# Attention with decay and two MLPs on one core: pairs 1 and 3 with p split in fp16, the low part of p's small row blocks on GpSimd, and v's bound by sums on ScalarE

## The chip, the cores and the metric

The kernel runs on one NeuronCore of a Trainium2 chip. The metric is the device time of one execution in microseconds (us), the median of several. Five engines work beside each other, each through its own queue in order: TensorE (PE in the profile; PEld is its weight load), VectorE (DVE), ScalarE (ACT), GpSimd (POOL) and SyncE (SP), which here only issues DMA transfers. An instruction that has to wait for another engine or a DMA holds up all that stands behind it on its own engine.

## The reference

```python
# q, k, v: (4 batches, 8 heads, 576 positions, 64); f: (4, 8, 576)
scores = q @ k.T / 8 + cum[:, None] - cum[None, :]     # cum: running sum of log f
attn   = softmax(causal(scores))                       # the kernel calls this p
x      = (attn @ v), heads side by side                # (2304, 512)
h      = x @ w_in;  g = max(h, 0) + alpha * min(h, 0); x = g @ w_out       # 512 -> 2048 -> 512
out    = ((x @ w_a) * (x @ w_b)) @ w_o                                     # 512 -> 1536 -> 512
```

## The kernel before

The 32 heads go through attention one after the other, two heads to a pair. A head's 576 rows of scores are four row blocks of 128 (numbered 0 to 3, with 128, 256, 384 and 512 columns because of the mask) and a rest of 64 rows, which both heads of a pair share (number 4, tile `sr`). A loop over u (line 645) goes through a list of operations: scores and softmax of head u (`s0` to `s3`, `R` for the rest), the scaling of p of head u - 1 by the softmax's sum (`h0` to `h4`) and what follows on it (`l0` to `l4`), and the products with v of head u - 2 (`p0`, `p1`). `T` makes q and k of head u + 1 ready, `vs` and `vm` work on v, `W` prepares one weight of the first MLP, and `M` takes a piece of the first MLP of an earlier batch. The MLP's matmuls are named h (with w_in) and y (with w_out); w_in and w_out come as 16 weights, one after the other through one raw tile `wr` and one tile `wx`: a DMA, then ACT (line 132), three operations on DVE (134 to 136), a cast on ACT and a subtraction on POOL.

From this list of operations a scheduler makes the order of every engine, from its own estimate of what is ready when. So a change of one operation moves others too.

Heads 0 to 9 (`NATIVE = 10`) work in f32: p is scaled in place (`p_hi`, line 461), PE transposes it block by block through PSUM (line 483), ACT and DVE copy the result out (line 237 or 235), and PE multiplies it with v in f32 (`pv_whole`, line 532). Heads 10 to 31 split p into two fp16 parts: POOL or ACT writes the high part (line 472 or 474), DVE the low part, s times ri minus the high part (line 554), DMAs transpose both (line 561), and PE multiplies them with v (lines 575 and 576), which was itself scaled and split into two fp16 parts by three operations of POOL (`split_v`, lines 325 to 327). The scale of v is one power of two for each batch, from a bound on v's absolute values: two loads of half a batch into one tile `vc` (line 334), DVE's maximum over each (line 338), and a chain over DVE, POOL (`vb`, line 345), PE (347) and DVE (348 to 353). Batch 0 is heads 0 to 7, all in f32, so this is done for batches 1 to 3 only, in the last three heads of the batch before.

Behind the heads, from about 378 us, come the rest of the first MLP and the second MLP.

Of the kernel before, what the change touches and what calls it, by code (L numbers as in the profile page):

```python
# [13 lines left out]
AF = mybir.ActivationFunctionType  # L14
ALU = mybir.AluOpType
# [33 lines left out]
    ws=[0, 1, 2, 3, 4, 5, 6, 7, 7, 8, 8, 9, 9, 10, 10, 11],  # L49
# [11 lines left out]
NATIVE = _P.get("native", 0)  # L61

# [24 lines left out]
def decay_attention_then_two_mlps(ctx, tc, q, k, v, f, w_in, w_out, alpha, w_a, w_b, w_o, out):  # L87
# [77 lines left out]
    ap_ = {"u": 0}  # L165
# [145 lines left out]
    def load_v(n):  # L311
        b, h = divmod(n, H)
        vs = ap_["vs", n % 3]
        i = 3 if n < NATIVE and n % 2 == 0 else 1
        sp.dma_start(vs[:, 0:4, i], v[b, h, 0:ST].rearrange("(t p) d -> p t d", p=128))
        sp.dma_start(vs[0:SR, 4, i], v[b, h, ST:])

    def split_v(n):

        if n < NATIVE:  # L320
            return
        vs = ap_["vs", n % 3]
        t = halves(n)
        scale = ap_["vm", (n // H) % 2][:, 1:2]
        pool.tensor_scalar(vs[:, :, 2], vs[:, :, 1], scale, 1.0, op0=ALU.mult, op1=ALU.mult)
        pool.tensor_scalar(t[:, :, 0:D], vs[:, :, 2], 1.0, 0.0, op0=ALU.mult, op1=ALU.add)
        pool.tensor_tensor(t[:, :, D:], vs[:, :, 2], t[:, :, 0:D], op=ALU.subtract)
# [8 lines left out]
    def batch_max(b, i):  # L336
        m = ap_["vm", b % 2][:, i:i + 1]
        dve.tensor_reduce(m, ap_["vc"], axis=mybir.AxisListType.X, op=ALU.max, apply_absolute_value=True)
# [55 lines left out]
    def s_view(n, i):  # L394
        if i == 4:
            return ap_["sr"]
        o = {3: 0, 2: 512, 1: 896, 0: 1152}[i]
        return ap_["s", n % 2][:, o:o + 128 * (i + 1)]
# [47 lines left out]
    p16 = {}  # L446

# [3 lines left out]
    def p_hi(n, i):  # L451

        g, o = GROUP[i]
        if n < NATIVE:
            s = s_view(n, i)
            ri = ap_["rir"][:, 0:1] if i == 4 else ap_["ri", n % 2][:, i:i + 1]
            e = eng(f"h{i}", "pool")
            if e is act:
                act.activation(s, s, AF.Copy, scale=ri)
            else:  # L460
                e.tensor_scalar(s, s, ri, 1.0, op0=ALU.mult, op1=ALU.mult)
            return
        if (n, g) not in p16:
            p16[n, g] = ap_["a"].tile(
                [128, GSIZE[g], 128], F16, tag=f"p16_{g}", name=f"p16_{n}_{g}", bufs=_P.get("p16", {}).get(g, 1),
            ), []
        t = p16[n, g][0][:, o:o + 2 * i + 2]
        s = s_view(n, i).rearrange("p (t n) -> p t n", n=128)
        ri = ap_["rir"][:, 0:1] if i == 4 else ap_["ri", n % 2][:, i:i + 1]
        e = eng(f"h{i}", "pool")  # L470
# [4 lines left out]
        p16[n, i] = t, s, ri  # L475

# [72 lines left out]
    def p_lo(n, i):  # L549
        if n < NATIVE:  # L550
            return p_whole(n, i)
        t, s, ri = p16.pop((n, i))
        g, o = GROUP[i]
        eng(f"l{i}", "dve").scalar_tensor_tensor(t[:, 1::2, :], s, ri, t[:, 0::2, :], op0=ALU.mult, op1=ALU.subtract)
        whole, done_ = p16[n, g]
        done_.append(i)
        if g == "r" or len(done_) == 2:
# [3 lines left out]
            sp.dma_start_transpose(out=PT[n, g], in_=whole.rearrange("p t n -> p (t n)"))  # L561
            del p16[n, g]

    def pv(u, c):

        if u < NATIVE:
            return pv_whole(u, c)
# [67 lines left out]
    def attention():  # L635
# [7 lines left out]
        load_qk(2)  # L643
        yield "W", -1
        for u in range(NI + LAG):
            ap_["u"] = u
            for op in order(u):
# [31 lines left out]
                elif op == "vm":  # L679
                    b = u // H + 1  # L680
                    if b < B and u % H >= H - 3:
                        i = u % H - (H - 3)
                        if i:
                            batch_max(b, i - 1)
                        if i < 2:
                            load_batch_v(b, i)
                        else:
# [430 lines left out]
```

## Time and profile before

| | us |
|---|---|
| median of 3 runs (lowest to highest) | 1076.65 (1076.21 to 1079.2) |
| profiled execution | 1079.26 |
| its span, first to last instruction | 1077.5 |

| engine | busy, share of the span |
|---|---|
| PE | 95% |
| PEld | 88% |
| DVE | 67% |
| POOL | 47% |
| ACT | 46% |

The profile is of one execution. Busy time is the time in which an engine has at least one instruction under way; matmuls overlap each other, so the duration of one is longer than its distance to the next. In the profile's names buffer numbers are left out.

### The profile page before, as it was taken

Reading aid. Unit: us, or ns where it says so; the run is one execution under the profiler, and the core shown is the slowest. Engines: PE = TensorE matmul, PEld = TensorE weight load, DVE = VectorE, ACT = ScalarE, POOL = GpSimd, SP = SyncE. Lnnn points to the kernel's source line nnn. Section 1 sums busy time; section 2 is a strip of 40 time slices with the busy share of each in tenths; the row PEclk is TensorE's granted clock in tenths of the full one; section 3 lists DMA queues with packets and bytes.
Section 4 is the critical chain, followed back from the end, with each engine's and each line's share of the span. In section 5 each row is a group of like instructions: output and inputs, shape, how many; then the busy total and the mean of one; then the engine's idle time right before and its main releaser. Section 6 shows DMA issues by size and latency. Waiting matters only on the chain.

```text
span 1077.5 us, 18303 instructions
## 1 busy us (share of the span) xinstructions
PE 1018.3 (95%) x6256; PEld 953.1 (88%) x6256; DVE 723.6 (67%) x1544; ACT 492.4 (46%) x1204; POOL 505.2 (47%) x593
## 2 busy tenths in 40 slices
PE   5899978999999999999999996999999999999998
PEld 3778868999988899999999995899989999899997
DVE  6667998698988836244467666755986558974553
ACT  6677776788777745333344443322433113321110
POOL 4334675576756745233356857522444224541111
PEclk9989988999999999999999998899999999999999
DMA  5655678596597485476767997626327383454623
GB/s 113 176 138 147 189 145 156 112 210 139 112 214 128 94 290 161 161 236 227 250 216 271 358 355 263 252 94 254 108 88 281 129 308 122 137 184 159 244 81 114
DMA packets 222561, 199.79 MB, mean 185 GB/s; under 512 B 139076, under 2 KB 195908, under 8 KB 222468
## 3 DMA queue, kind: packets, MB, share of 16 engines
q1 hardware_dynamic: 222468, 198.62, 61.0%
q8 instruction: 49, 0.80, 0.3%
q14 instruction: 44, 0.36, 0.1%
HBM read 130.37 MB, written 50.17 MB: 168 GB/s over the span
## 4 chain that ended last, share of the span: by engine, by line
PE 50%; DVE 7%; issue 3%; DMA 3%; POOL 2%; ACT 2%; DVEq 0%; ACTq 0%; POOLq 0%; SPq 0%
PE p L710 7%; PE p L712 7%; PE p L711 7%; PE o L712 4%; PE o L711 4%; PE o L710 4%; PE ya L711 3%; PE hb L712 3%; PE hb L710 3%; PE hb L711 3%; PE ya L712 3%; PE ya L710 3%; DMA wr_in<-in_moe_w_in 1%; POOL yhl L917 1%; DVE wx_a L135 1%
## 5 line engine op out<-in xcount | busy, mean ns | idle before, releaser
L710 PE MATMUL p<-yq,w_h 128*128 128x384 f32 x360 | 122.7, 341 | 7.9 <-ACT w_h L140 6.4
L711 PE MATMUL p<-yq,w_h 128*128 128x384 f32 x360 | 122.2, 339 | 0.0
L712 PE MATMUL p<-yq,w_h 128*128 128x384 f32 x360 | 121.5, 338 | 0.0
L1051 POOL TENSOR_TENSOR gg<-tc,gg 128x384 fp32r<-128x384 f32 x36 | 37.0, 1028 | 113.6 <-ACT gg L1050 103.3
L710 PE MATMUL o<-w_o,gg 128*128 128x512 f32 x216 | 84.8, 394 | 4.7 <-ACT gg L1050 4.7
L711 PE MATMUL o<-w_o,gg 128*128 128x512 f32 x216 | 85.1, 394 | 0.0
L712 PE MATMUL o<-w_o,gg 128*128 128x512 f32 x216 | 84.5, 395 | 0.0
L420 ACT ACTIVATE s<-s,nm 128x512 f32<-128x512 f32 (+3 forms) x128 | 71.4, 558 | 21.7 <-DVE nm L419 21.4
L1051 POOL TENSOR_TENSOR gg<-td,gg 128x384 fp32r<-128x384 f32 x36 | 37.2, 1035 | 93.7 <-ACT gg L1050 88.0
L710 PE MATMUL h<-xh,w_in 128*128 128x288 f32 x256 | 77.4, 306 | 2.8 <-DVE lt L705 2.8
L707 POOL TENSOR_TENSOR gb<-lt,gb 128x384 fp32r<-128x384 f32 x48 | 50.0, 1042 | 63.6 <-ACT gb L706 63.6
L710 PEld LDWEIGHTS p<-yq,w_h 128*128 128x128 f32 x360 | 68.1, 189 | 12.4 <-ACT w_h L140 6.9
L710 PE MATMUL y<-g,w_out 128*128 128x288 f32 x256 | 77.1, 306 | 1.1 <-DVE lt L705 0.9
L711 PE MATMUL y<-g,w_out 128*128 128x288 f32 x256 | 76.2, 300 | 1.2 <-POOL g L707 1.2
L705 DVE SCALAR_TENSOR_TENSOR lt<-lu,nal,hb 128x384 f32<-128x384 f32 x48 | 29.3, 611 | 70.8 <-ACT lu L704 69.2
L712 PE MATMUL h<-xh,w_in 128*128 128x288 f32 x256 | 75.5, 296 | 0.0
L711 PE MATMUL h<-xl,w_in 128*128 128x288 f32 x256 | 75.4, 295 | 0.0
L712 PE MATMUL y<-g,w_out 128*128 128x288 f32 x256 | 75.0, 299 | 0.0
L1050 ACT CAST gg<-tc 128x384 fp32r<-128x384 f32 x36 | 18.5, 514 | 123.4 <-DVE tc L1049 122.9
L711 PEld LDWEIGHTS p<-yq,w_h 128*128 128x128 f32 x360 | 68.2, 189 | 3.5
L419 DVE CUSTOM_DVE_ANT_0 s<-sc,maskz 128x512 f32<-128x512 f32 (+3 forms) x128 | 59.8, 485 | 16.2 <-PE sc L403 14.1
L712 PEld LDWEIGHTS p<-yq,w_h 128*128 128x128 f32 x360 | 67.8, 188 | 0.2
(216 smaller groups left out, 3261.6 us busy)
## 6 DMA issues: line engine op xcount, KB each, us to landing
yq<-yq_d SPq DMA_DIRECT2D x49, 768.0 KB
yq_d<-yhl SPq DMA_DIRECT2D x42, 384.0 KB
yl<-ya_d SPq DMA_DIRECT2D x48, 192.0 KB
po_d<-os SPq DMA_DIRECT2D x36, 256.0 KB
os<-po_d SPq DMA_DIRECT2D x36, 256.0 KB
wr_in<-in_moe_w_in SPq DMA_DIRECT2D x16, 512.0 KB
wr_out<-in_moe_w_out SPq DMA_DIRECT2D x16, 512.0 KB
wr_a<-in_moe_w_a SPq DMA_DIRECT2D x12, 512.0 KB
```

What stands on the lines that cost most here:

```text
L135: dve.scalar_tensor_tensor(x, high, -2 ** 31, x, op0=ALU.bitwise_and, op1=ALU.bitwise_or)
L419: dve.tensor_tensor_reduce(s, o, m, -0.125, 3.0e38, ALU.add, ALU.min, nm)
L420: act.activation(s, s, AF.Exp, bias=nm, scale=-1.0, accum_out=sm)
L705: dve.scalar_tensor_tensor(t, u, nal[:, fi:fi + 1], hp[:, :n], op0=ALU.mult, op1=ALU.add)
L707: pool.tensor_tensor(gl, t, f32(gh), op=ALU.subtract)
L710: pe.matmul(o, lh, rh, start=start, stop=False)
L711: pe.matmul(o, lh, rl, start=False, stop=False)
L712: pe.matmul(o, ll, rh, start=False, stop=stop)
L917: pool.tensor_tensor(yh[:, 1], x, f32(yh[:, 0]), op=ALU.subtract)
L1050: ap_["last"] = act.copy(g[:, 0], o).ins
L1051: pool.tensor_tensor(g[:, 1], o, f32(g[:, 0]), op=ALU.subtract)
```

## The change

Five edits. `whole(n)` says which heads stay in f32: of the first ten now only pairs 0, 2 and 4 (heads 0, 1, 4, 5, 8, 9), while pairs 1 and 3 (heads 2, 3, 6, 7) take p and v in fp16; their scores stay in f32. In all heads that are split, the low part of row blocks 0 and 1 goes from DVE to POOL: POOL scales both in place (two operations, as before, but written to s), copies both at once to the high part (384 columns) and subtracts both at once; s is laid out so that the two blocks lie side by side. The bound on v is now the sum of absolute values along each row, made by ACT (1152 columns with an accumulated sum, in place), not a maximum on DVE. Batch 0 gets one too, loaded ahead of the loop and finished in the first two heads. And the second weight of step 7 moves to step 8, with the later ones behind it.

```diff
-    ws=[0, 1, 2, 3, 4, 5, 6, 7, 7, 8, 8, 9, 9, 10, 10, 11],
+    ws=[0, 1, 2, 3, 4, 5, 6, 7, 8, 8, 9, 9, 10, 10, 11, 11],
...
+def whole(n):
+
+    return n < NATIVE and n // 2 % 2 == 0
...
     def split_v(n):
 
-        if n < NATIVE:
+        if whole(n):
             return
...
-    def batch_max(b, i):
-        m = ap_["vm", b % 2][:, i:i + 1]
-        dve.tensor_reduce(m, ap_["vc"], axis=mybir.AxisListType.X, op=ALU.max, apply_absolute_value=True)
+    def batch_bound(b, i):
+        c = ap_["vc"]
+        act.activation(c, c, AF.Abs, accum_out=ap_["vm", b % 2][:, i:i + 1])
...
-        o = {3: 0, 2: 512, 1: 896, 0: 1152}[i]
+        o = {3: 0, 2: 512, 0: 896, 1: 1024}[i]
...
+        if g == "lo":
+            pool.tensor_scalar(s, s, ri, 1.0, op0=ALU.mult, op1=ALU.mult)
+            p16[n, i] = None
+            low_done[n] = low_done.get(n, 0) + 1
+            if low_done[n] == 2:
+                dup(pool, p16[n, g][0][:, 0::2, :], lo_view(n))
+            return
...
+    def lo_view(n):
+        return ap_["s", n % 2][:, 896:1280].rearrange("p (t n) -> p t n", n=128)
...
-        eng(f"l{i}", "dve").scalar_tensor_tensor(t[:, 1::2, :], s, ri, t[:, 0::2, :], op0=ALU.mult, op1=ALU.subtract)
...
+        if g != "lo":
+            t, s, ri = got
+            dve.scalar_tensor_tensor(t[:, 1::2, :], s, ri, t[:, 0::2, :], op0=ALU.mult, op1=ALU.subtract)
+        elif len(done_) == 2:
+            pool.tensor_tensor(parts[:, 1::2, :], lo_view(n), parts[:, 0::2, :], op=ALU.subtract)
...
         stack(0)
         warm_up(_P.get("wu", [0, 0])[1], "b")
         load_qk(2)
+        load_batch_v(0, 0)
...
-                    b = u // H + 1
-                    if b < B and u % H >= H - 3:
-                        i = u % H - (H - 3)
-                        if i:
-                            batch_max(b, i - 1)
-                        if i < 2:
+                    for b in range(B):
+                        i = u - 8 * b + 3 if b else u + 1
+                        if i in (1, 2):
+                            batch_bound(b, i - 1)
+                        if i in (0, 1):
                             load_batch_v(b, i)
```

What the scheduler makes of it shows at three places. In the names the first number is the head (s_0 and s_1 are the two tiles of scores, used in turn). First ACT at the start, behind the softmax of head 0: the scaling of its row block 2, the rest's exponential (sr), the copy of the transposed p (PT32), the copies of q and k of head 2 (N_0), and head 1's exponentials. Before:

```order
L459 ACTIVATE s_0_151<-s_0_151,ri_0_154 128x384
L439 ACTIVATE sr_164,smr_167<-sr_164,nmr_166 128x576
L235 COPY PT32_0_hi_283<-tp_0_2_0_284 128x3x128
L235 COPY N_0_103<-tqk_2_0_290 64x288 x2
L235 COPY N_0_103<-tqk_2_1_296 64x288 x2
L420 ACTIVATE s_1_160,sm_1_162<-s_1_160,nm_1_161 128x512
L132 ACTIVATE wx_in0_252<-wr_in0_250 128x512
```

And now, to the same exponential of head 1 (vc's sums are those with 1152 columns):

```order
L344 ACTIVATE vc_178,vm_0_180<-vc_178 128x1152
L445 ACTIVATE sr_164,smr_167<-sr_164,nmr_166 128x576
L138 ACTIVATE wx_in0_255<-wr_in0_253 128x512
L344 ACTIVATE vc_178,vm_0_180<-vc_178 128x1152
L146 CAST w_in0_260<-wx_in0_255 128x512
L241 COPY PT32_0_hi_296<-tp_0_2_0_297 128x3x128
L241 COPY N_0_103<-tqk_2_0_303 64x288 x2
L241 COPY N_0_103<-tqk_2_1_309 64x288 x2
L138 ACTIVATE wx_in1_348<-wr_in1_346 128x512
L241 COPY PT32_0_lo_330<-tp_0_0_0_331 128x384
L344 ACTIVATE vc_178,vm_1_181<-vc_178 128x1152
L426 ACTIVATE s_1_160,sm_1_162<-s_1_160,nm_1_161 128x512
```

Three sums over vc, two weights' first steps and a cast now stand ahead of head 1's first exponential. On PE at the same place (scr: the rest's scores, tp: transposes of p, tqk: transposes of q and k), now:

```order
L409 MATMUL scr_1_1_271<-N_1_108 128x288
L353 MATMUL vm_0_289<-ident_90,vb_179 128x128
L498 MATMUL tp_0_2_0_297<-ident_90,s_0_151 128x128 x3
L378 MATMUL tqk_2_0_303<-ident_90,qkn_2_198 128x96 x3
L378 MATMUL tqk_2_1_309<-ident_90,qkn_2_198 128x96 x3
L498 MATMUL tp_0_3_3_315<-ident_90,s_0_151 128x128 x4
L409 MATMUL sc_1_3_321<-N_1_108 128x512
```

The second row, the transpose of batch 0's bound, is the new one; the others stood in the same order before. The second place is POOL in head 25's step, with p of head 24 and v of head 25 (vs). Before:

```order
L474 TENSOR_SCALAR p16_24_hi_3869<-s_0_151,ri_0_154 128x4x128
L474 TENSOR_SCALAR p16_24_lo_3872<-s_0_151,ri_0_154 128x128
L474 TENSOR_SCALAR p16_24_lo_3872<-s_0_151,ri_0_154 128x2x128
L325 TENSOR_SCALAR vs_1_172<-vs_1_172,vm_1_181 128x5x64
L326 TENSOR_SCALAR vs_1_172<-vs_1_172 128x5x64
L327 TENSOR_TENSOR vs_1_172<-vs_1_172 128x5x64
```

And now:

```order
L475 TENSOR_SCALAR s_0_151<-s_0_151,ri_0_154 128x128
L475 TENSOR_SCALAR s_0_151<-s_0_151,ri_0_154 128x256
L486 TENSOR_SCALAR p16_24_hi_3918<-s_0_151,ri_0_154 128x4x128
L245 TENSOR_SCALAR p16_24_lo_3921<-s_0_151 128x3x128
L575 TENSOR_TENSOR p16_24_lo_3921<-s_0_151,p16_24_lo_3921 128x3x128
L331 TENSOR_SCALAR vs_1_172<-vs_1_172,vm_1_181 128x5x64
L332 TENSOR_SCALAR vs_1_172<-vs_1_172 128x5x64
L333 TENSOR_TENSOR vs_1_172<-vs_1_172 128x5x64
```

Two rows more, and they stand ahead of v's. The third place is PE around the widest scores of head 16 (sc_16_3), with the first MLP's second matmuls (y, the first number is the batch, the second the half of it). Before:

```order
L711 MATMUL y_0_288_0_2280<-g_0_288_1895,w_out5_1365 128x288
L712 MATMUL y_0_288_0_2280<-g_0_288_1895,w_out5_1365 128x288
L710 MATMUL y_0_288_0_2280<-g_0_288_1895,w_out6_1375 128x288
L406 MATMUL sc_16_3_2353<-U1_0_147,T1_0_146 128x512
L407 MATMUL sc_16_3_2353<-TU2_0_148 128x512
```

And now:

```order
L412 MATMUL sc_16_3_2403<-U1_0_147,T1_0_146 128x512
L413 MATMUL sc_16_3_2403<-TU2_0_148 128x512
L729 MATMUL y_0_0_0_1611<-g_0_0_1259,w_out7_1593 128x288
L730 MATMUL y_0_0_0_1611<-g_0_0_1259,w_out7_1593 128x288
L729 MATMUL y_0_0_1_1696<-g_0_0_1259,w_out7_1593 128x288
```

At this point the MLP was in the second half of batch 0 and is now still in the first, at its last weight, w_out7; the order has it nearly level again at head 18 (408 of the MLP's matmuls ahead of that head's widest scores before, 404 now).

## Rows read from the trace of the kernel before

**Rows 1.** Stretches (us): length, busy (x instructions) by engine, granted clock, DMA share, GB/s.

```profile
14.00:108.00 94.00, 85.00 (x488) 68.66 (x486) 62.06 (x194) 66.85 (x181) 32.24 (x46) 0.95 0.59 156
108.00:152.00 44.00, 38.32 (x284) 35.48 (x283) 40.43 (x114) 34.20 (x101) 31.93 (x45) 1.00 0.68 174
152.00:175.00 23.00, 18.15 (x108) 15.41 (x108) 20.33 (x58) 16.76 (x45) 13.47 (x19) 0.63 0.75 152
175.00:220.00 45.00, 43.24 (x358) 41.99 (x357) 33.29 (x92) 30.52 (x87) 27.19 (x41) 1.00 0.65 131
220.00:378.00 158.00, 149.29 (x1248) 140.92 (x1246) 135.27 (x370) 121.65 (x343) 108.48 (x160) 1.00 0.70 148
378.00:1077.00 699.00, 680.75 (x3774) 648.79 (x3772) 422.88 (x702) 216.77 (x439) 281.88 (x256) 0.99 0.59 206
```

**Rows 2.** Timeline, 15 to 25 us: start, length, engine, line, operation, idle before.

```profile
15.76 2.61 SPq L222 DMA_DIRECT2D cum_d<-rows  x4
...
19.68 0.59 SPq L128 DMA_DIRECT2D wr_in<-in_moe_w_in  x1
...
19.68 0.55 PE L483 MATMUL tp<-ident,s 128*128 128x128 f32 x3 [0.59 <-ACT s L459]
...
22.80 0.72 ACT L420 ACTIVATE s<-s,nm 128x512 f32<-128x512 f32 x1
...
24.51 0.66 ACT L132 ACTIVATE wx_in<-wr_in 128x512 f32<-128x512 f32 x1 [0.89 <-DMA wr_in<-in_moe_w_in]
```

**Rows 3.** Timeline, 38 to 52 us: loads of vc and their readers.

```profile
38.48 0.59 SPq L334 DMA_DIRECT2D vc<-in_v  x1
...
45.09 1.35 DVE L338 TENSOR_REDUCE vm<-vc 128x1 f32<-128x1152 f32 x1 [0.54 <-DMA vc<-in_v]
...
46.47 0.35 SPq L334 DMA_DIRECT2D vc<-in_v  x1
...
50.70 1.35 DVE L338 TENSOR_REDUCE vm<-vc 128x1 f32<-128x1152 f32 x1 [1.22 <-DMA vc<-in_v]
```

**Rows 4.** Timeline of PE: f32 head at 34 us, fp16 head at 254 us.

```profile
34.12 0.93 PE L483 MATMUL tp<-ident,s 128*128 128x128 f32 x7
34.88 2.11 PE L403 MATMUL scr<-N 128*128 128x288 f32 x8
36.82 0.82 PE L532 MATMUL pvw<-PT_lo,vs 128*128 128x256 f32 x4
37.48 1.68 PE L532 MATMUL pvw<-PT_hi,vs 128*128 128x256 f32 x8
38.99 1.23 PE L532 MATMUL pvw<-PT_r,vs 128*128 128x64 f32 x10
...
253.92 0.28 PE L575 MATMUL pv<-PT_lo,vs 128*128 128x256 f16 x1
...
255.65 0.38 PE L710 MATMUL y<-g,w_out 128*128 128x288 f32 x1
```

**Rows 5.** Groups, 110:390: count, busy, mean ns; last row: ns least, median, most.

```profile
L554 DVE SCALAR_TENSOR_TENSOR p_lo<-s,ri,p_lo 128x128 f16<-128x128 f32 x22 | 12.2, 554 | 0.4 <-POOL p_lo L474 0.3
L554 DVE SCALAR_TENSOR_TENSOR p_lo<-s,ri,p_lo 128x256 f16<-128x256 f32 x22 | 12.1, 550 | 0.0
L327 POOL TENSOR_TENSOR vs<-vs 128x320 f16<-128x320 f32 x22 | 18.8, 855 | 1.2
L326 POOL TENSOR_SCALAR vs<-vs 128x320 f16<-128x320 f32 x22 | 11.0, 501 | 1.2
...
L554 DVE SCALAR_TENSOR_TENSOR p_lo<-s,ri,p_lo x44: 331/487/1137, 131.3 to 374.9; 128x128 f16<-128x128 f32 x22, 128x256 f16<-128x256 f32 x22
```

**Rows 6.** Waits of PE, 110:385: us in total, times, longest.

```profile
PE h L710 <- DVE lt L705: 2.8, 4, 1.8
PE pv L575 <- DVE nm L419: 2.8, 6, 0.6
```

**Rows 7.** Timeline of DVE: the first softmax step of head 9.

```profile
108.30 0.69 DVE L419 CUSTOM_DVE_ANT_0 s<-sc,maskz 128x512 f32<-128x512 f32 x1
```

More of the change, by code (lines that the diff above doesn't have):

```diff
@@ L313, in load_v @@
         vs = ap_["vs", n % 3]
-        i = 3 if n < NATIVE and n % 2 == 0 else 1
+        i = 3 if whole(n) and n % 2 == 0 else 1
         sp.dma_start(vs[:, 0:4, i], v[b, h, 0:ST].rearrange("(t p) d -> p t d", p=128))
@@ L446, in decay_attention_then_two_mlps @@
     p16 = {}
+    low_done = {}
     GROUP = {0: ("lo", 0), 1: ("lo", 2), 2: ("hi", 0), 3: ("hi", 6), 4: ("r", 0)}
@@ L453, in p_hi @@
         g, o = GROUP[i]
[L454 to L457, printed above, removed]
+        s = s_view(n, i)
+        ri = ap_["rir"][:, 0:1] if i == 4 else ap_["ri", n % 2][:, i:i + 1]
+        e = eng(f"h{i}", "pool")
+        if whole(n):
             if e is act:
@@ L466, in p_hi @@
             ), []
+        if g == "lo":
[5 more added lines that the diff above has]
+            return
         t = p16[n, g][0][:, o:o + 2 * i + 2]
-        s = s_view(n, i).rearrange("p (t n) -> p t n", n=128)
-        ri = ap_["rir"][:, 0:1] if i == 4 else ap_["ri", n % 2][:, i:i + 1]
-        e = eng(f"h{i}", "pool")
+        s = s.rearrange("p (t n) -> p t n", n=128)
         if e is act:
@@ L549, in p_lo @@
     def p_lo(n, i):
-        if n < NATIVE:
+        if whole(n):
             return p_whole(n, i)
-        t, s, ri = p16.pop((n, i))
         g, o = GROUP[i]
-        eng(f"l{i}", "dve").scalar_tensor_tensor(t[:, 1::2, :], s, ri, t[:, 0::2, :], op0=ALU.mult, op1=ALU.subtract)
-        whole, done_ = p16[n, g]
+        parts, done_ = p16[n, g]
         done_.append(i)
+        got = p16.pop((n, i))
+        if g != "lo":
[3 more added lines that the diff above has]
+            pool.tensor_tensor(parts[:, 1::2, :], lo_view(n), parts[:, 0::2, :], op=ALU.subtract)
         if g == "r" or len(done_) == 2:
@@ L560, in p_lo @@
             )
-            sp.dma_start_transpose(out=PT[n, g], in_=whole.rearrange("p t n -> p (t n)"))
+            sp.dma_start_transpose(out=PT[n, g], in_=parts.rearrange("p t n -> p (t n)"))
             del p16[n, g]
     def pv(u, c):
-        if u < NATIVE:
+        if whole(u):
             return pv_whole(u, c)
@@ L679, in attention @@
                 elif op == "vm":
-                    b = u // H + 1
-                    if b < B and u % H >= H - 3:
-                        i = u % H - (H - 3)
-                        if i:
-                            batch_max(b, i - 1)
-                        if i < 2:
+                    for b in range(B):
[3 more added lines that the diff above has]
+                        if i in (0, 1):
                             load_batch_v(b, i)
-                        else:
+                        if i == 2:
                             batch_scale(b)
```

## The prediction

> **What bounds the kernel now.** I read the table of stretches first [rows 1]. TensorE (PE) is busy 681 of the last 699 us, which the change leaves alone, and 85 of 94 us in the stretch of the first ten heads. So PE sets the end, and a change pays by taking work from PE or by closing its gaps. The gaps lie ahead of 220 us: 9.0 us in 14:108, 5.7 in 108:152, 4.9 in 152:175 at a granted clock of 0.63 (between the two levels 1.2 and 2.4 GHz), and 8.7 in 220:378. In that last stretch VectorE (DVE) is busy 86% and in 108:152 92%, more than any other engine beside PE, and where PE waits behind 110 us, DVE is named eight times in the list, with the MLP's lt and the softmax's nm ahead [rows 6]. In 14:108 it is another picture: DVE 66%, ScalarE (ACT) 71%, GpSimd (POOL) 34%.
>
> **The change part by part.** All sums are against the profiled execution, span 1077.5 us, 1079.26 with what lies around it. The median of the runs is 1076.65, 2.6 less, so I carry the difference over to the median.
>
> *1. v's bound for the first batch, at the start.* Pairs 1 and 3 need v scaled, so batch 0 needs a bound, and its chain now stands ahead of head 0's transposes on PE and ahead of their evictions on ACT, as the pieces above show. I follow it by rows. The first load of vc takes the place on the DMA queue where the four cum_d issues began, 15.76 [rows 2]. From issue to its reader such a load took 6.61 us once (38.48 to 45.09) and 4.23 another time (46.47 to 50.70) [rows 3]. I take 4.2, as the start has less traffic, and keep 6.6 as the end. So ACT can read at 20.0. The sum of 1152 columns isn't in the trace: the nearest row is the exponential of 512 columns with its sum, 0.72 [rows 2], which scaled up gives 1.6, and 0.72 itself is the lower end; I take 1.5. The second load goes into the same tile, so it is issued at 21.5, lands at 25.7 and is summed by 27.2. DVE's maximum, POOL's vb and PE's transpose of it add some 1 us. Head 0's transposes, at 19.68 now [rows 2], then begin at 28.2: 8.5 us later, by 6.6-us loads 13.
>
> It goes on behind that. The first weight took from its issue at 19.68 to ACT's read at 24.51, 4.8 us [rows 2]. Its successor shares the one raw tile, so it is issued when DVE is done with the first (about 27.5) and is read at 32.3. ACT's row for it now stands ahead of head 1's exponentials, and so does the third load of vc (batch 1's), which is issued only after vb is read, at about 28.5 to 30, and is summed at 34 to 36. Head 1's first exponential, at 22.80 now [rows 2], comes at about 36. PE has nothing else to do in that time. Term: **+13**, bounds +8.5 (what stands behind catches up) and +18 (both long loads).
>
> *2. Pairs 1 and 3 in fp16.* Off PE per head: ten transposes and half of a pair's five, at 0.109 us (seven in 34.12 to 34.88), 1.36 us; and the f32 products with v, 0.66 + 1.51 + 1.23 = 3.40 us [rows 4]. On PE per head: the fp16 products of a head, from 253.92 to 255.65, 1.73 us with two products of the MLP (some 0.35 us) between them, so 1.38 us [rows 4]. Four heads: 4 x (1.36 + 3.40 - 1.38) = 13.5 us. It is not all kept, since the other engines have to go faster to let PE use it. From head 1's exponential (22.80) to head 9's first softmax (108.30 [rows 7]) are 85.5 us. ACT's share of 71% makes 61 us of work there, and about four of the seven new sums that stand ahead of head 9's softmax fall behind head 1's, 6 us: 67 us. In 72 us that would be 93% of an engine that works in order, in 77 us 87%, which is what DVE reaches in 220:378. So I credit 9 us of it. Term: **-9**, bounds 0 and -13.5. POOL's additions in these heads (three operations on v, the subtractions for x) lie in an engine that is idle for two thirds; if that cover were gone they would cost what stands in part 3.
>
> *3. The low part of row blocks 0 and 1.* DVE loses 44 operations behind 108 us, 12.2 + 12.1 = 24.3 us [rows 5], 1.1 us per head. POOL gets two operations on 384 columns per head; by the 320-column ones of 0.855 and 0.501 us [rows 5] they cost 1.03 + 0.60 = 1.6 us, 36 us in 22 heads. POOL is busy 181 of the 270 us from 108 to 378 [rows 1], so it comes to 80%. In 220:378 fourteen heads free 15 us of DVE against PE's 8.7 us of gaps. DVE is not the releaser of all of them (a DMA, ACT and POOL are others), so I take **-5** there, bounds 0 and -8.7. In 108:152 three split heads free 3.3 us of DVE, but one weight more is prepared there: **-2**, bounds +1 and -4.
>
> The shared port speaks against this part. On DVE the low parts took 331 ns at best, 487 in the middle and 1137 at worst, and the mean of 128 columns is no less than that of 256 (554 and 550 ns) [rows 5], so something other than their size makes them long. The Trainium skill, SBUF — State Buffer, section Who interferes with whom, says that a DVE instruction with two inputs in SBUF contends with a GpSimd instruction that reads SBUF and that the second to issue waits until the first is done. The spread fits that rule, though no row here shows who was met. By it POOL's 1.6 us more per head of SBUF reading meets the large low parts that stay on DVE; the change removes two meetings per head and lengthens others, and where the rule takes all, the term is rival D.
>
> *4. Weights and the first MLP's second half.* In the changed order the products with w_out7 stand behind head 16's first score, in the old one 142 products of the MLP stand ahead of it; before, the thin heads are 13 and 14, now 13 to 15. The stretch 152:175 is such heads: 4.85 us idle, and at a clock of 0.63 another 18.15 x 0.37 = 6.7 us, so 5.8 per head. One more thin head is +5.8; thin heads run at DVE's pace, which is 1.1 us shorter for each of three. Term: **+3**, bounds 0 and +6.
>
> Sum: 13 - 9 - 5 - 2 + 3 = 0. The change moves the time by about nothing: a long stall is bought at the start and paid back piece by piece.
>
> **The rivals.**
> B, the stall is paid back in full. For it: PE's 13.5 us are certain, and PE was the fullest engine in 14:108. Against it: ACT's 93%. With +10 for the start, -13.5 for PE, -10 for part 3 and 0 for part 4 the sum is -13.5: 1063 us.
> C, ACT becomes the bound of the first ten heads. Place: ACT's queue, where each sum waits for a load of vc and each weight for its DMA with exponentials queued behind, and DVE's softmax and PE's scores wait for those. For it: the rows of head 1 above; against it: ACT's idle 29% now. Price: start +15, only 4 of the 13.5 us kept, -3 in the later heads, +4 in the thin ones, together +12: 1088.5 us. It decides from the point where ACT is over some 90% busy between the starts of heads 1 and 9.
> D, what DVE gains behind 108 us is lost to the shared port or to POOL's longer queue, ahead of the MLP's subtractions. The two terms of part 3 go to 0: 1083.5 us. For it: the maxima of the low parts; against it: POOL at 80%, not above.
>
> **How the numbers follow.** A, the forecast, 0.46: 1076.5 us, its own range 1070 to 1083. B 0.27 (1060 to 1070), C 0.17 (1081 to 1094), D 0.10 (1079 to 1086). A change under 0.3% (3.2 us) can't be told from none, so faster is below 1073.4, slower above 1079.9. Faster: 0.26 from B and 0.10 of A, 0.36. Slower: 0.16 from C, 0.08 from D and 0.08 of A, 0.32. Same: 0.32. The range 1064 to 1088 leaves out half of B and some of C.
>
> **What would show it.** Part 1: the first transposes of p on PE near 28 us, waiting for vb, and head 1's first exponential of 512 columns near 36; near 24 the stall was hidden. Part 2: head 9's first softmax near 112; at 105 rival B, at 116 or later with ACT over 90% rival C. Part 3: DVE under 80% and POOL near 80% in the late heads, PE's gaps there near 4 us; if they stay at 9 and DVE's remaining low parts are longer, rival D. Part 4: a low clock for about three heads around 165 us, and a block of MLP products ahead of head 18. The forecast is wrong if the start of head 9 and the start of head 18 both move the same way by over 6 us.

## The result, and the profile after

| | before | after |
|---|---|---|
| median of the runs, us (lowest to highest) | 1077.93 (1076.21 to 1080.08) | 1090.33 (1088.94 to 1092.31) |
| span of the profiled execution, us | 1077.5 | 1088.7 |

The ratio is 1.0115, 95% interval 1.0088 to 1.0142: slower by 1.2%, outside the range of 1064 to 1088 that I gave. (A fourth run of the kernel before moved its median from the 1076.65 us that the prediction starts from to 1077.93.) First the stretches of the kernel after, to be held against [rows 1]; the columns are the same.

```profile
14.00:108.00 94.00, 71.63 (x418) 55.01 (x417) 61.74 (x196) 72.32 (x188) 48.84 (x67) 0.91 0.76 182
108.00:152.00 44.00, 36.00 (x247) 32.87 (x245) 36.36 (x95) 31.52 (x92) 30.38 (x42) 0.88 0.79 187
152.00:175.00 23.00, 17.67 (x120) 14.99 (x121) 21.29 (x51) 17.65 (x47) 17.98 (x24) 0.85 0.64 150
175.00:220.00 45.00, 39.67 (x285) 35.90 (x285) 36.53 (x95) 31.38 (x86) 40.61 (x55) 0.89 0.71 145
220.00:378.00 158.00, 153.40 (x1279) 147.14 (x1278) 118.59 (x337) 120.11 (x344) 121.48 (x182) 1.00 0.67 148
378.00:1088.00 710.00, 690.56 (x3858) 658.04 (x3855) 430.00 (x717) 222.50 (x454) 291.06 (x267) 0.99 0.60 204
```

PE has 13 us less to do in the first stretch, and 220:378 is what was meant: PE busy 97%, DVE 75%, POOL 77%. The loss is in the three rows between. There before had a low clock in 152:175 only; after, PE is at 0.85 to 0.89 through all of 108:220 and idle 18.7 us there (12.3 before).

The first softmax step of a head (DVE's 128x512 step of that head) is a clock for the attention:

| head | 1 | 5 | 9 | 12 | 15 | 18 | 21 | 31 |
|---|---|---|---|---|---|---|---|---|
| before, us | 22.1 | 68.4 | 108.3 | 138.9 | 174.4 | 220.1 | 253.8 | 365.5 |
| after, us | 35.3 | 70.2 | 107.3 | 149.2 | 182.2 | 233.6 | 266.4 | 375.4 |

The stall is there at head 1 and gone at head 9. It is lost again between heads 9 and 18, and 3.6 us come back by head 31. The row for head 9, against [rows 7]:

```profile
107.26 0.69 DVE L425 CUSTOM_DVE_ANT_0 s<-sc,maskz 128x512 f32<-128x512 f32 x1
```

The start, against [rows 2]: PE's timeline and ACT's sums of batch 0 (the bracket is the idle time before, and who ended it).

```profile
30.38 0.47 PE L353 MATMUL vm<-ident,vb 128*128 128x128 f32 x1 [11.61 <-POOL vb L351]
30.65 0.85 PE L498 MATMUL tp<-ident,s 128*128 128x128 f32 x3
```

```profile
20.05 1.16 ACT L344 ACTIVATE vc<-vc 128x1152 f32<-128x1152 f32 x1 [0.53 <-DMA vc<-in_v]
28.39 1.16 ACT L344 ACTIVATE vc<-vc 128x1152 f32<-128x1152 f32 x1 [1.91 <-DMA vc<-in_v]
```

PE stands 11.6 us for the small tile vb that the two loads and sums end in. Now the row that I should have looked up before predicting: POOL's last step on the last of the 16 weights of the first MLP phase, before and after.

```profile
169.96 1.28 POOL L141 TENSOR_TENSOR w_out<-wx_out,w_out 128x512 fp32r<-128x512 f32 x1 [2.47 <-ACT w_out L140]
```

```profile
192.92 1.27 POOL L147 TENSOR_TENSOR w_out<-wx_out,w_out 128x512 fp32r<-128x512 f32 x1
```

Each output of the first MLP's second half sums over all eight blocks of w_out, so until then the MLP has little for PE: 61.7 us behind head 9 before, 85.7 after. I call that distance the **lag**. What PE loses I take from windows of 2.5 us: its idle time, and its busy time times (1 - granted clock).

| us | PE's work at full clock, 14 to head 9 | lost | work, head 9 to 21 | lost | work, 21 to 31 | lost |
|---|---|---|---|---|---|---|
| before | 81.1 | 13.3 | 126.2 | 19.4 | 104.9 | 6.8 |
| after | 66.6 | 26.7 | 128.6 | 30.5 | 104.5 | 4.6 |

By differences: -14.5 + 13.4 + 2.4 + 11.1 - 0.4 - 2.2 = +9.8, which is the shift of head 31 (+9.9); +1.3 more comes behind it. The 2.4 of work I can't place; it may come from the windows' averaging of the clock, which no run shows.

### The profile page after: what moved, and what is told of

Same layout as the page of the kernel before. It is cut to its first block, busy times and chain, and to the rows that moved or that the text cites. A ratio compares the mean times of both kernels' runs of the same rounds, so it can differ in the third digit from the quotient of the medians.

```text
span 1088.7 us, 18278 instructions
## 1 busy us (share of the span) xinstructions
PE 1012.3 (93%) x6207; PEld 945.9 (87%) x6207; DVE 713.4 (66%) x1506; ACT 501.1 (46%) x1220; POOL 560.3 (51%) x662
## 4 chain that ended last, share of the span: by engine, by line
PE 63%; DVE 10%; POOL 5%; issue 4%; ACT 2%; DMA 1%; SPq 0%; POOLq 0%; DVEq 0%; ACTq 0%
PE p L729 7%; PE p L731 7%; PE p L730 7%; PE o L731 4%; PE o L730 4%; PE o L729 4%; PE ya L730 3%; PE hb L731 3%; PE hb L729 3%; PE hb L730 3%; PE ya L731 3%; PE ya L729 3%; PE y L730 2%; PE y L729 2%; PE y L731 2%
## 5 line engine op out<-in xcount | busy, mean ns | idle before, releaser
L1070 POOL TENSOR_TENSOR gg<-tc,gg 128x384 fp32r<-128x384 f32 x36 | 37.0, 1027 | 113.6 <-ACT gg L1069 103.3
L729 PE MATMUL y<-g,w_out 128*128 128x288 f32 x256 | 78.5, 311 | 1.7 <-ACT g L725 0.9
L730 PE MATMUL y<-g,w_out 128*128 128x288 f32 x256 | 77.9, 306 | 0.8 <-POOL g L726 0.8
L731 PE MATMUL y<-g,w_out 128*128 128x288 f32 x256 | 75.4, 302 | 2.9 <-POOL w_out L147 2.9
L1069 ACT CAST gg<-tc 128x384 fp32r<-128x384 f32 x36 | 18.5, 514 | 123.4 <-DVE tc L1068 122.9
L730 PEld LDWEIGHTS p<-yq,w_h 128*128 128x128 f32 x360 | 67.9, 188 | 3.5
```

The lines of the kernel that those rows point to most:

```text
L729: pe.matmul(o, lh, rh, start=start, stop=False)
L730: pe.matmul(o, lh, rl, start=False, stop=False)
L731: pe.matmul(o, ll, rh, start=False, stop=stop)
L1069: ap_["last"] = act.copy(g[:, 0], o).ins
L1070: pool.tensor_tensor(g[:, 1], o, f32(g[:, 0]), op=ALU.subtract)
```

## The experiments

All ratios are against the kernel before, run beside each (1075.8 to 1077.9 us); the scheduler puts the first 220 us in a new order with every edit of the order, so no edit is quite alone. The time is the median of several runs, the columns behind the ratio are of the one profiled run; that run was 4.2 us under the median in x1 (1076.6) and 4.7 above it in x2 (1068.5, the longest of six). Measured in all of them (us; ready: start of POOL's step on the last w_out; lost: between heads 9 and 21, as above):

| run | time | ratio, 95% interval | head 9 | ready | lag | lost | head 21 |
|---|---|---|---|---|---|---|---|
| before | 1077.93 | 1 | 108.3 | 170.0 | 61.7 | 19.4 | 253.8 |
| after | 1090.33 | 1.0115, 1.0088 to 1.0142 | 107.3 | 192.9 | 85.7 | 30.5 | 266.4 |
| u1_bound_dve | 1091.39 | 1.0124, 1.0108 to 1.0140 | 116.1 | 185.3 | 69.2 | 25.1 | 270.4 |
| u2_ws | 1088.31 | 1.0104, 1.0091 to 1.0118 | 108.0 | 188.2 | 80.2 | 28.6 | 264.5 |
| u3_low_dve | 1102.45 | 1.0233, 1.0217 to 1.0250 | 111.7 | 209.0 | 97.3 | 38.7 | 277.6 |
| u4_whole | 1079.80 | 1.0025, 1.0010 to 1.0039 | 105.7 | 186.3 | 80.6 | 24.9 | 258.8 |
| v1_chain_only | 1079.10 | 1.0018, 1.0003 to 1.0033 | 114.5 | 169.7 | 55.2 | 14.7 | 256.4 |
| v2_split_only | 1078.71 | 1.0019, 1.0003 to 1.0035 | 96.2 | 182.3 | 86.1 | 29.6 | 254.0 |
| v3_low_only | 1080.80 | 1.0034, 1.0020 to 1.0048 | 106.7 | 179.7 | 73.0 | 25.6 | 258.6 |
| v4_act_sums_only | 1083.22 | 1.0055, 1.0036 to 1.0075 | 105.4 | 182.0 | 76.6 | 25.3 | 259.1 |
| w1_weights_early | 1081.36 | 1.0051, 1.0039 to 1.0063 | 117.4 | 164.7 | 47.4 | 13.6 | 259.4 |
| w2_before_weights_late | 1082.28 | 1.0056, 1.0039 to 1.0074 | 105.6 | 185.0 | 79.4 | 27.4 | 260.8 |
| w3_scale_late | 1083.28 | 1.0066, 1.0054 to 1.0078 | 104.2 | 190.4 | 86.2 | 30.9 | 263.1 |
| w4_scale_late_weights_early | 1090.78 | 1.0135, 1.0122 to 1.0148 | 108.3 | 185.3 | 77.0 | 27.8 | 265.9 |
| x1_weights_on_act_queue | 1080.75 | 1.0022, 1.0005 to 1.0039 | 113.1 | 158.5 | 45.3 | 17.1 | 256.5 |
| x2_before_two_raw | 1063.79 | 0.9866, 0.9841 to 0.9892 | 103.3 | 151.0 | 47.8 | 18.5 | 246.9 |
| x3_before_two_raw_low | 1067.60 | 0.9905, 0.9886 to 0.9924 | 102.0 | 149.9 | 47.9 | 14.1 | 243.2 |
| x4_split_two_raw | 1076.95 | 0.9994, 0.9982 to 1.0007 | 98.6 | 172.6 | 74.0 | 27.0 | 256.3 |
| y1_split_two_raw_act_queue | 1067.00 | 0.9896, 0.9878 to 0.9914 | 101.5 | 152.1 | 50.6 | 16.4 | 246.1 |
| y2_before_two_raw_act_queue | 1065.39 | 0.9891, 0.9875 to 0.9907 | 103.2 | 125.5 | 22.3 | 13.1 | 243.3 |

### One part undone

u1_bound_dve:

```diff
-        act.activation(c, c, AF.Abs, accum_out=ap_["vm", b % 2][:, i:i + 1])
+        dve.tensor_reduce(ap_["vm", b % 2][:, i:i + 1], c, axis=mybir.AxisListType.X, op=ALU.max, apply_absolute_value=True)
```

> The changed kernel with one part undone: v's bound is again a maximum taken by VectorE (eight reductions of some 1.35 us) in place of the eight sums of 1.35 us on ScalarE. Theory W (ScalarE's sums and the transfers that they release early push the weight chain back, so that the last quarter of w_out is ready at 193 us in place of 170, and the MLP can't fill heads 13 to 17): the instruction order puts 357 MLP matmuls ahead of head 17's first scores in place of 204, as before the change, so the last w_out is ready near 175 us and 8 to 13 us come back: 1077 to 1082. Theory P (GpSimd's extra work on the low part binds heads 12 to 18): GpSimd's work is untouched and VectorE gets 11 us more, so 1089 to 1094. Theory S (the split of pairs 1 and 3 and the stall at the start cost it): both are still there, 1088 to 1092.

No change, so theory W missed here: the weight was ready at 185, not 175, though the order had its products early. The loss behind head 9 fell by 5.4, but head 9 came 8.8 later; 3.9 of that is there at head 1 already (39.2), behind the start's chain with its maxima on DVE. It doesn't tell the theories apart.

u2_ws:

```diff
-    ws=[0, 1, 2, 3, 4, 5, 6, 7, 8, 8, 9, 9, 10, 10, 11, 11],
+    ws=[0, 1, 2, 3, 4, 5, 6, 7, 7, 8, 8, 9, 9, 10, 10, 11],
```

> The changed kernel with the table of weight places as it was before the change (w_out 0 to 6 asked for one place earlier). Theory W: the order has the last w_out after head 14's exponentials in place of head 15's, and 228 MLP matmuls ahead of head 17 in place of 204; with 0.13 us a matmul that is 3 us, so 1086 to 1089. If the table were the whole of the delay the time would go back to 1078. Theories P and S: no change, 1090 +- 2.

1 to 2 us, as W had it, but the intervals overlap. The table's shift by itself is not the cause.

u3_low_dve (in `p_hi` the branch for "lo" goes, in `p_lo` POOL's subtraction):

```diff
-        if g != "lo":
+        if True:
             t, s, ri = got
             dve.scalar_tensor_tensor(t[:, 1::2, :], s, ri, t[:, 0::2, :], op0=ALU.mult, op1=ALU.subtract)
```

> The changed kernel with the low part of the two small row blocks made by VectorE again, from s, with GpSimd rounding the high part as before the change. Theory P: GpSimd is rid of some 1.9 us a head, heads 12 to 18 go back to before's pace, 1076 to 1081. Theory W: the order has only 204 MLP matmuls ahead of head 19, where the changed kernel has 456, so the MLP is later still, and VectorE gets 0.91 us a head back: 1092 to 1100. Theory S: 1090 and VectorE's 0.2 us a head over heads 18 to 31, 1091 to 1095.

Slower by 12 us, not faster, and above W's range: P, the overload of POOL, falls for this kernel. The last weight came at 209 and the loss rose with it.

u4_whole:

```diff
-    return n < NATIVE and n // 2 % 2 == 0
+    return n < NATIVE
...
-        load_batch_v(0, 0)
...
-                    for b in range(B):
-                        i = u - 8 * b + 3 if b else u + 1
+                    for b in range(1, B):
+                        i = u - 8 * b + 3
```

> The changed kernel with all ten first heads' p whole in fp32, as before the change, so that batch 0 needs no bound and no load of it; the sums on ScalarE, the low part on GpSimd and the later weights stay. Theory S (split and start stall are the cost): 1076 to 1080. Theory W: the start stall is gone but the order still has 204 MLP matmuls ahead of head 18 (404 in the changed kernel, 408 before), the last w_out after head 15's exponentials: 1088 to 1096. Theory P: GpSimd's work in heads 10 to 31 stays, 1088 to 1092.

S was right: the split of pairs 1 and 3, with the chain that it needs, costs some 10 us. W as I had put it was wrong: the places in the scheduler's order do not tell the time.

### The chain and the split apart, and two parts alone

v1_chain_only (the first edit of u4_whole alone):

```diff
-    return n < NATIVE and n // 2 % 2 == 0
+    return n < NATIVE
```

> The changed kernel with all ten first heads' p whole in fp32, but with batch 0's load, its two sums and its scale still made at the start (nothing reads the scale): the chain at the start without the split that needs it. The same kernel without that chain took 1079.8 us. Theory C (the chain at the start is the cost: TensorE stands 13 us before head 1): 1088 to 1092. Theory D (the split of pairs 1 and 3 is the cost, through what it puts on VectorE, GpSimd and the DMA queue while the weights are made): 1078 to 1083, with head 1's first softmax still at 35 us. Theory W by the instruction order alone (252 MLP matmuls ahead of head 15 in place of 150, the last w_out after head 12's exponentials): 1075 to 1085.

v2_split_only (the other edits of u4_whole, and):

```diff
+        dve.memset(ap_["vm", 0][:, 1:2], 2.0 ** 5)
+        dve.memset(ap_["vm", 0][:, 2:3], 2.0 ** -20)
```

> The changed kernel with batch 0's load, sums and scale left out: a constant scale of 2^5 stands in for the one worked out, so pairs 1 and 3 are split as in the changed kernel and the start has no chain. Theory C: 1078 to 1082, head 9's first softmax 8 to 13 us sooner than the changed kernel's 107.3. Theory D: 1086 to 1092, since the last w_out still comes late. Theory W by the order alone (159 MLP matmuls ahead of head 17, 408 ahead of head 18; last w_out after head 16's exponentials): the MLP is as late, 1084 to 1092.

The chain alone costs nothing (1.0018 against 1.0025 with neither), the split alone costs nothing (1.0019), both together 1.0115. So theories C and D both fall: the two parts cost something only together. v2 shows also what the split buys: head 9 at 96.2, 9.5 us sooner than u4_whole, and next to nothing of it left at the end: the last w_out came only 4.0 sooner and the loss grew by 4.7. v1 has the opposite: head 9 is 8.8 later, but the weights used the stall: the last w_out came 16.6 sooner, the lag is 55 and the loss 10.2 less.

Two differences say it more simply. Between v1 and u4 the stall is 12.9 us at head 1 and paid back by head 21 (2.4 sooner). Between after and v2, with the split in both, it is 13.1 at head 1 and still 12.6 at head 31, the last w_out comes 10.6 later and the loss is about the same (30.5 and 29.6). With the split nothing pays the stall back, and most of what the split itself gains up to head 9 is lost behind it, in v2 as in after.

v3_low_only (the kernel before with the change's `p_hi`, `p_lo`, `lo_view` and score places, no more):

```diff
+        elif len(done_) == 2:
+            pool.tensor_tensor(parts[:, 1::2, :], lo_view(n), parts[:, 0::2, :], op=ALU.subtract)
```

> The kernel before with only the low part of the two small row blocks given to GpSimd (and its places in the score tile). Theory P (GpSimd overloaded): 1080 to 1088. The other: the third run above showed the changed kernel 12 us slower with this part undone, and VectorE gives up 0.91 us a head here, so 1066 to 1073; the order's 165 MLP matmuls ahead of head 16 (307 before) would take some of it back, 1070 to 1076.

From head 21 to 31 it gains 2.9 us (111.7 to 108.8), as part 3 of the prediction would have it, and from head 9 to 21 it loses 6.4: the last weight is 10 us later. The time lies at the lower end of P's range and above the other's, so the low part on POOL, with the new order that it brings, does cost something here; the weights' loads are issued no later than before (late by 5.0 us in sum, 4.9 before; the sum is explained below), but from a load's issue to DVE's last step on it the sixteen take 153 us, 144 before.

v4_act_sums_only:

```diff
-        dve.tensor_reduce(m, ap_["vc"], axis=mybir.AxisListType.X, op=ALU.max, apply_absolute_value=True)
+        act.activation(ap_["vc"], ap_["vc"], AF.Abs, accum_out=m)
```

> The kernel before with only v's bound of batches 1 to 3 taken by ScalarE's sums. Theory W: the order has 204 MLP matmuls ahead of head 17 (357 before), the last w_out one place later: 1080 to 1088. By engine work alone (six reductions of 1.35 us leave VectorE, ScalarE has them instead, VectorE being the busier of the two): 1073 to 1078.

As W expected, 6 us slower by the ratio, with the last weight 12 us later.

### The weights alone

w1_weights_early:

```diff
-    ws=[0, 1, 2, 3, 4, 5, 6, 7, 8, 8, 9, 9, 10, 10, 11, 11],
+    ws=[0, 0, 1, 1, 2, 3, 3, 4, 5, 5, 6, 7, 7, 8, 8, 9],
```

> The changed kernel with the table of weight places moved ahead (0, 0, 1, 1, 2, 3, 3, 4, 5, 5, 6, 7, 7, 8, 8, 9); nothing else. Theory W, with the size that the runs so far give it: what TensorE loses between head 9's and head 21's first softmax (idle, and busy at a low clock) was 14.7, 19.3, 24.9 and 30.5 us where the last w_out was ready 55, 62, 81 and 86 us behind head 9, some half a microsecond for each. The order now has the last w_out after head 12's exponentials (15 in the changed kernel); if it is ready near 172 us, 65 behind head 9 at 107, the loss falls by about 10 us and the time to 1077 to 1082. Theory I (the split and the chain collide in the first 100 us in some other way, on SP's queue or GpSimd): the time stays, 1087 to 1091.

The weight came 28 us sooner and the loss fell by 17, more than expected; head 9 came 10 later; the weights' work may now hold up the first heads, among which it stands. By the ratios 7 of the 12 us are back.

w2_before_weights_late:

```diff
-    ws=[0, 1, 2, 3, 4, 5, 6, 7, 7, 8, 8, 9, 9, 10, 10, 11],
+    ws=[0, 1, 2, 3, 4, 5, 6, 7, 8, 9, 10, 11, 11, 12, 12, 13],
```

> The kernel before with its table of weight places moved back (w_out 1 to 7 asked for at heads 9, 10, 11, 11, 12, 12, 13), so that the order has the last w_out after head 15's exponentials and 168 MLP matmuls ahead of head 17, as in the changed kernel (15 and 204); nothing else. Theory W: head 9 stays at 108, the last w_out is ready at 185 to 193 in place of 170, and the loss grows by 8 to 11 us: 1084 to 1089. If late weights alone cost nothing: 1076 to 1079.

This is the step of the prediction by itself, in the kernel before: a last w_out 15 us later makes the loss 8.0 larger and the kernel 0.56% slower. The time lies under W's range; head 9 came 2.7 sooner, and the kernel before took 1075.8 beside it.

w3_scale_late:

```diff
-                        if i == 2:
+                        if i == 2 and b:
...
+                if op == "l4" and u == 1:
+                    batch_scale(0)
```

> The changed kernel with batch 0's scale written at the end of head 1's work, so that its transpose lies behind head 0's transposes and head 1's scores on TensorE; nothing else. The stall of 12 us at the start should go: head 1's first softmax at 22 to 27 us in place of 35.3, head 9's at 97 to 100. Theory W: the last w_out (after head 14's exponentials in the order) comes at 182 to 188, the loss stays near 28 us, and half of the 9 us at head 9 is kept: 1081 to 1086. If the stall were the cost as such, all of it comes back: 1077 to 1080.

Head 1 is back at 22.5, but most of the wait moved: head 2 is at 33.7 (27.5 before) and head 9 at 104, not at 97 to 100. The time lies where W put it.

w4_scale_late_weights_early: the edits of w1 and w3.

> Both edits of the last two runs together: batch 0's scale behind head 1's scores, and the table of weight places moved ahead. Order: last w_out after head 14's exponentials, 357 MLP matmuls ahead of head 17. Theory W: head 9 near 98, last w_out near 175, so the sum of the two falls by 27 us against the changed kernel, half of which is 13 us: 1074 to 1080, the best of the four. Theory I: no better than the run before it, 1081 to 1088.

A miss for both theories: the two edits don't add. The scheduler's order had the last w_out after head 14's exponentials; on the chip it was ready at 185. What held is the loss at that lag, 27.8 at 77.

Over the 19 kernels with a lag above 40 us the loss follows the lag with 0.41 us per us (correlation 0.96, none off the line by over 3.6); at a lag of 22 (y2) 13 us are left. That the one causes the other is best shown by w1 and w2, whose only edit is the table of weight places.

### The queue and the raw tile

Why did the weights not use the stall once the split was there? One reason is SyncE's queue. Its timeline of the kernel after, behind the moment (54.87 + 1.29 us) at which DVE had done with the raw tile of the fourth weight:

```profile
54.87 1.29 DVE L142 SCALAR_TENSOR_TENSOR wx_in<-wr_in,wx_in 128x512 int32<-128x512 int32 x1
```

```profile
55.63 1.35 SPq L580 DMA_TRANSPOSE PT_lo<-p_lo  x1
57.10 1.54 SPq L580 DMA_TRANSPOSE PT_hi<-p_hi  x1
59.37 1.33 SPq L580 DMA_TRANSPOSE PT_r<-p_r  x1
60.79 0.65 SPq L372 DMA_DIRECT2D N<-cum_d  x1
61.50 0.41 SPq L134 DMA_DIRECT2D wr_in<-in_moe_w_in  x1
```

The tile is free at 56.2 and the load issued at 61.5; for 4.3 of the 5.3 us between, the queue is taken by three transposes of p of pair 1 and a load of cum_d. The same two steps in the kernel before, where nothing stands between them:

```profile
55.41 0.74 DVE L136 SCALAR_TENSOR_TENSOR wx_in<-wr_in,wx_in 128x512 int32<-128x512 int32 x1
56.22 0.38 SPq L128 DMA_DIRECT2D wr_in<-in_moe_w_in  x1
```

Without the split there are no such transposes this early; with the split and no stall (v2) this load is 0.6 us late. Over the fifteen links the load was issued 19.5 us in sum after its tile was free, in v2 5.8, in the kernel before 4.9. In 14.8 of the 19.5 us another issue was under way, in 10.4 a transpose.

The queue is not the whole reason. From v1 to after the last w_out comes 23.3 us later: 9.3 of that are late issues (10.2 in v1), and 16.4 the sixteen weights' time from a load's issue to DVE's last step on it (133.0 in v1, 149.4 after; 154.3 in v2, 153.5 in u4); what follows on the last weight is 2.5 shorter. What makes these steps so short in v1 alone was not tried. And w4 has late issues of 4.1 us only, with its last w_out at 185 all the same.

x1_weights_on_act_queue:

```diff
-        sp.dma_start(raw.rearrange("p c e t -> p c (e t)"), w_src[kind](i))
+        act.dma_start(raw.rearrange("p c e t -> p c (e t)"), w_src[kind](i))
```

> The changed kernel with the weights' transfers issued by ScalarE's queue in place of SyncE's; nothing else. In the changed kernel a weight's load was issued 19 us in sum later than its raw tile came free (4 us in the kernel before), most of it where it stood on SyncE behind the transposes of p of pair 1. Theory Q (SyncE's queue, in which the late transposes of pairs 1 and 3 stand ahead of the weight loads, makes the weights late): the last w_out at 165 to 178 in place of 193; by half a microsecond each that is 7 to 13 us, with up to 10 us back at head 9 where the weights then crowd it, as in the run with the early table: 1076 to 1085. Rival (the chain is late for its four steps on ScalarE, VectorE and GpSimd): the last w_out stays past 185, 1087 to 1092.

The time is as Q had it: the sum of late issues is 2.6 us, the chain from first to last weight 144 us in place of 163, and 10 us of the 12.4 are back. But the run moves two things: the first load now also goes out at 0.7 us, 19.6 sooner than in after, which is part of why the last w_out is as early as 158.5 (sooner than Q's 165 to 178) and goes with a longer start (head 1 at 39.4). What each of the two is worth the run does not tell. The Trainium skill, DMA: Bandwidth & Descriptors, section Issuing engines are not separate DMA queues, says that DMAs of all issuing engines run on the same 16 DMA engines and interleave, which no run here shows; its section Rules for kernel authors adds that spreading them over engines only saves issue time. Here the issue of a load is 0.4 us; what the move took away are 17 us in sum in which the loads stood behind other issues.

x2_before_two_raw:

```diff
-        raw = mp["stage"].tile([128, C, 128, 2], I32, tag="wraw", name=f"wr_{kind}{i}")
+        raw = mp["stage"].tile([128, C, 128, 2], I32, tag="wraw", name=f"wr_{kind}{i}", bufs=2)
...
-VC = H * S * D // 256
+VC = H * S * D // 512
...
-        dve.tensor_tensor(m, m, scale, op=ALU.max)
+        dve.tensor_reduce(m, t, axis=mybir.AxisListType.X, op=ALU.max)
...
```

> The kernel before with two tiles for the raw weights in place of one (the next transfer starts while the last is worked on); to make room v's bound is read in four quarters of a batch in place of two halves. Theory W: each of the fifteen links of the chain loses up to the 4.8 us of its transfer, the last w_out comes at 130 to 150 in place of 170 and the loss between heads 9 and 21 falls from 19 to 10 us or less, with 5 to 10 us back at head 9: 1068 to 1076. If the chain is bound by the engines' order: 1075 to 1079.

1.3% faster than before, and by the two ratios 2.5% than after (0.9866 / 1.0115): the lowest ratio, though the intervals of x3, y1 and y2 reach into this one. The reason is only half of what I expected. The stretches:

```profile
14.00:108.00 94.00, 88.14 (x518) 71.72 (x517) 67.89 (x216) 72.97 (x198) 38.12 (x51) 0.96 0.70 186
108.00:152.00 44.00, 37.60 (x245) 35.69 (x244) 38.42 (x97) 28.22 (x79) 28.11 (x37) 0.84 0.48 114
152.00:175.00 23.00, 22.32 (x191) 21.47 (x190) 19.66 (x52) 17.73 (x51) 15.58 (x23) 1.00 0.64 138
```

The thin place is over by 152 (the last w_out is ready 19 us sooner than before), but the loss behind head 9 is hardly less (18.5). In the profiled run, 5 of the 10.8 us of the span are won ahead of head 9, where I expected a price, and 1.9 each between heads 9 and 21, 21 and 31, and behind. Why the first heads gain was not tried further.

x3_before_two_raw_low: x2 with the edits of v3 and the table of w1.

> The run before this one with the low part of the two small row blocks on GpSimd and the weight table moved ahead. Theory W: the low part on GpSimd took 2.9 us off heads 21 to 31 in the kernel before and lost 6.4 between heads 9 and 21 with a last w_out 10 us later; with early weights only the gain is left: 3 us below the run before it, 1065 to 1073. Theory P (GpSimd's extra work costs by itself): no better than it or slower, 1075 to 1081.

Its heads are ahead of x2's (head 31 at 354.0, 356.6 there), its time is not (0.9905 against 0.9866): the 3 us that I expected of the low part on POOL did not show, and x2's heads are those of its longest run.

x4_split_two_raw: v2 with the second raw tile and the quarters of x2.

> The changed kernel without batch 0's chain at the start (a constant scale of 2^5 in its place) and with two tiles for the raw weights and v's bound of the other batches in quarters. It took 1078.7 with one raw tile, head 9 at 96.2 and the last w_out at 182. Theory W: the order has the last w_out after head 13's exponentials in place of head 16's; if it is ready near 160, the loss of 29.6 us falls by 10 and the time to 1066 to 1073, the shortest yet. If the engines' order binds the chain: 1076 to 1080.

W's number missed. The last w_out only moved to 172.6: with the split, a second raw tile is not enough while the loads share SyncE's queue. They are issued 27.0 us late in sum, 5.0 of it under transposes and 9.1 under loads of q and k.

y1_split_two_raw_act_queue: x4 with the edit of x1. y2_before_two_raw_act_queue: x2 with the edit of x1.

> The run of the split with two raw tiles (1077.0 us; constant scale of 2^5 for batch 0, so no chain at the start) with the weight loads issued by ScalarE's queue as well. Theory W: there the last w_out came at 172.6, 74 behind head 9; the order has it after head 12's exponentials now (13 before), as early as in the kernel before with two raw tiles. If it is ready near 150, the loss of 27 us between heads 9 and 21 falls by some 10 and the split's work saved is kept: 1062 to 1070. If the split slows the weights by its work on VectorE and GpSimd whatever the queue: 1074 to 1079.

> The kernel before with two raw tiles (1063.8 us) with the weight loads issued by ScalarE's queue. Its chain hardly waited for SyncE, the last w_out lies 48 us behind head 9 already, and the loss stopped falling below some 50 us in the runs so far, while the weights crowd the start: no gain, 1062 to 1070. If earlier weights still paid: 1056 to 1061.

Both as W had them. Off SyncE the split's weights come at 152 and it takes 10 us less than x4; in the kernel without the split the loads were late by only 6.6 us in sum (x2), and although the last w_out now comes 25.5 sooner, nothing is gained. Even so the split is not ahead of x2. Up to head 9 PE has 12.7 us less to do there than in x2 (67.9 against 80.6 at full clock) and loses 10.9 more (19.6 against 8.7).

## Why the prediction was wrong, step by step

*Step 1, the stall:* right. Transposes at 28.2 forecast, 30.65 measured; head 1 later by 13.3.

*Step 2, pairs 1 and 3:* PE's saving right (13.5 forecast, 14.5 measured). I credited 9 of it for fear of ACT at 93%; ACT was at 84% from head 1 to head 9 (60.4 of 71.9 us), all of it was used, and head 9 came at 107.3, not 112. Up to there the split's saving covered the stall, as rival B had it.

*Step 3, the low part:* right in its own rows of the late heads; 3.6 of its 5 us came back between heads 18 and 31. Its 2 us in 108:152 did not come: PE is idle 8.0 us there, 5.7 before, which belongs to step 4. POOL's two new operations, and the large low parts left on DVE, against [rows 5] (columns as there, behind 108 us):

```profile
L575 POOL TENSOR_TENSOR p_lo<-s,p_lo 128x384 f16<-128x384 f32 x22 | 21.9, 997 | 0.6
L245 POOL TENSOR_SCALAR p_lo<-s 128x384 f16<-128x384 f32 x22 | 13.7, 622 | 5.0 <-DMA PT_lo<-p_lo 4.5
```

```profile
L573 DVE SCALAR_TENSOR_TENSOR p_hi<-s,ri,p_hi 128x384 f16<-128x384 f32 x22 | 18.4, 835 | 4.4 <-ACT p_hi L484 4.2
```

35.6 us on POOL where I had 36; PE's loss from head 21 to 31 down to 4.6, where I had said near 4. The last row is longer than before. The rule that rival D took from the Trainium skill, SBUF — State Buffer, section Who interferes with whom, that a DVE instruction with two SBUF inputs contends with GpSimd's reads, would make it so, though no row shows what these operations met. Before, it was

```profile
L554 DVE SCALAR_TENSOR_TENSOR p_hi<-s,ri,p_hi 128x384 f16<-128x384 f32 x22 | 16.0, 726 | 4.2 <-ACT p_hi L472 3.9
```

So 2.4 us in 22 operations; the larger two forms grew by 8 and 9 ns. D did not decide.

*Step 4, the weights:* **this one failed.** "+3, bounds 0 and +6"; from head 9 to head 18 the kernel lost 14.6 us where steps 3 and 4 together had +1. The mechanism was right (thin heads at a low clock while the MLP waits for w_out), its size was not. I counted in the scheduler's order which heads stand ahead of the last weight (13 and 14, now 13 to 15) and paid one head. But the order is no clock: u1, u4 and w4 have the weight at other places and come out otherwise than these say. What sets the price is when the last w_out is ready, 23 us later, at 0.4 to 0.5 us each: the loss between heads 9 and 21 rose by 11.1. Of the 23, 14.6 are late issues in SyncE's queue (19.5 against 4.9), 5.1 longer steps on the weights. I had followed the moved DMAs at the start only, and had not asked whom the new transposes stand in front of. w2 shows the step alone in the kernel before, w1 takes back 7 of the 12 us by earlier weights alone, x1 10. The sign that I had named, heads 9 and 18 both over 6 us off the same way, could not catch this: head 9 came 1.0 sooner and head 18 13.5 later.

Rival C came near the number (1088.5) by luck, by a cause that did not happen: ACT stayed under 90% and head 9 was early.

## What to carry to other kernels

Where filler work waits for data of its own, look up when its last input is ready, and price a change by how it moves that time against the work that needs filling; heads gained ahead of it were worth half or nothing here. When an edit adds DMAs to a queue, list the issues that stand behind them: here two edits, each free alone, cost 1% together, in part because the transposes of the one, made late by the other, stood in front of the weight loads. In the kernel before, a second buffer for the longest prefetch chain was worth 1.3%, and the arithmetic that the change moves between engines won nothing.

## What the runs showed of the hardware

The clock falls where PE is thin and stays low while PE is already full again. The kernel after, three stretches:

```profile
115.00:120.00 5.00, 3.04 (x20) 2.67 (x19) 4.35 (x14) 4.63 (x14) 3.36 (x6) 0.84 0.84 271
120.00:125.00 5.00, 5.00 (x21) 4.61 (x21) 4.25 (x10) 2.85 (x10) 3.64 (x6) 0.50 1.02 347
125.00:130.00 5.00, 5.00 (x38) 4.84 (x37) 4.92 (x17) 4.28 (x11) 3.53 (x6) 0.98 1.02 323
```

PE was busy 3.0 of 5 us, then all of 5 at 0.50, the lower of its two levels (1.2 of 2.4 GHz), with 21 matmuls where the next 5 us hold 38. So a thin head costs its idle time and then some more: 11.4 of the 30.5 us lost between heads 9 and 21 are low clock, not idleness. And a transpose by DMA holds the queue that issues it three times as long as a weight load (0.4 us): ns least, median and most of the 22 of PT_lo,

```profile
L580 SPq DMA_TRANSPOSE PT_lo<-p_lo x22: 1211/1244/2021, 133.8 to 388.2; - x22
```
